# Attention and mixture of experts on one core: unit loads cut in two and tied to places of TensorE's step, two pieces of the routing moved on VectorE

## The chip, the cores and the metric

The kernel runs on one core of one Trainium2 chip. The metric is the device time of one execution in microseconds (us). Before the change three runs took 606.4, 601.0 and 603.85 us, a median of 603.85 us. The profiled execution took 600.04 us, and its span from the first to the last instruction is 598.2 us.

## The reference

The reference has two halves. The first is attention for batch 8, 8 heads, sequence 576 and head size 64, in float32. Heads 0 to 3 look at a local window (the last 32 positions), heads 4 to 7 at a strided set (earlier positions with the same remainder by 32). The second is a mixture of 8 experts over the 4608 tokens: logits from a gate matrix and a bias by modality, the expert with the largest logit, its softmax weight, and a two-layer network with ReLU.

```python
rel = pos[:, None] - pos[None, :]
mask_local = (rel >= 0) & (rel < stride)
mask_strided = (rel >= 0) & (pos[None, :] % stride == pos[:, None] % stride)
...
logits = x @ w_gate + modality_bias[modality_id]
e_idx = np.argmax(logits, axis=1)
...
h = np.maximum(x[mask] @ w1[e], 0.0)
out[mask] = gate_w[mask, None] * (h @ w2[e])
```

## The kernel before

**Attention.** The work is cut into 32 units that alternate between `Local` (one local head of two batches) and `Strided` (two strided heads of one batch). A software pipeline at L1093 to L1122 runs step n over them. In step n TensorE gets, in an order written out by hand (`tc.manual_schedule` for PE): the scores of unit n, the turn (transposes) of unit n-2, the masks of unit n+1 and the values of unit n-3. The `prep` of unit n+2 (L306, L400: copies of the queries into a padded tile on VectorE and ScalarE, pinned in program order) comes after that. After a batch pair's eight units, `finish_pair` and `route` are generators from which `pop(POPS)` takes five pieces a step; what a piece gives TensorE stands between the steps. Each pair's routing thus falls into the steps of the next pair. The last pair's falls into the expert stage.

**Loads.** All unit loads are issued from SP. A `Local` unit has one load of 592 KB for queries and keys (`qk`, L296) and one of 585 KB for values (`vv`, L301); a `Strided` unit has 576 KB (`qks`, L390) and 288 KB (`vs`, L395). Query and key tiles have two buffers for each kind of unit, so the load of unit n+3 can start when the scores of unit n-1 are done. The values of unit n-1 wait, from n = 3 on, for the last transpose of unit n-3 (`point`, L1099). The scheduler may move these loads on SP, except the first values, which are pinned.

**Routing.** `route` adds up logits on TensorE (L523, L528), turns them (L537), and then on VectorE finds the largest logit and the one-hot expert (L549 to L564). ScalarE takes the exponentials (L565), VectorE their sum and its reciprocal (L567, L568, L571) and a scan (L575). After 11 pieces TensorE computes ranks (`rk`, L579), VectorE the positions (L582 to L586), the expert counts (`new`, `fst`, `stp`, `cnt`, L588 to L594) and one-hot tables (L604). GpSimd multiplies `hv` (L613), and TensorE gathers the entry table (`en`, L619). Engines other than TensorE get their order from the scheduler's own timeline, except where instructions are pinned.

**Experts.** From step 28 on, GpSimd looks up entries (L810), gathers tokens (L793) and weights (L825) in a fixed order of transfers. The first slot's tokens are transposed after step 33 (L1121, `turn(0)`, L217). Twelve slots of 384 tokens and a half slot then run two layers on TensorE (L957, L971).

Of the kernel before, what the change touches and what calls it, by code (L numbers as in the profile page):

```python
# [38 lines left out]
FILL = {2: 4, 3: 6}  # L39
SETUP = 6  # L40
POPS, POPF = 5, 3
LT, RK = 7, 11
LAG = 2
PLANE, SEND, SPLIT, TURN = 1, 3, 6, 4
WHEN = {1: 0, 3: 1, 5: 2, 7: 3}
# [138 lines left out]
def attention_moe(ctx: ExitStack, tc: tile.TileContext, a, out):  # L184
# [72 lines left out]
    fst = cp.tile([P, NBP, E], BF16, name="fst")  # L257
    stp = cp.tile([P, NBP, E], BF16, name="stp")

    outs = _Group(tc, "outs")  # L260
    pace = [None]

# [24 lines left out]
    class Local:  # L287
# [2 lines left out]
        def __init__(self, bp, h, xt):  # L290
            self.bp, self.h, self.xt, self.n = bp, h, xt, 4 * bp + h

        def load(self):
            n = self.n
            self.qk = lp.tile([P, 37, 32], F32, tag="qk", name=f"qk{n}")
            nc.sync.dma_start(self.qk.rearrange("p i q -> p (i q)"), a["qkl"][self.bp, self.h])  # L296

        def load_values(self):
            n = self.n
            self.vv = lp.tile([P, 18, D + 1], F32, tag="vv", name=f"vv{n}")  # L300
            ins = nc.sync.dma_start(self.vv.rearrange("p i c -> p (i c)"), a["vl"][self.bp, self.h])  # L301
            if n < 2:
                pin(ins)
            return ins

        def prep(self):  # L306
            self.qd = qd = qds[self.n % 2]
# [12 lines left out]
        def scores(self):  # L320
            n, qk, qd = self.n, self.qk, self.qd
            mx = lp.tile([P, 9], F32, tag="mx", name=f"mx{n}")
            self.ex = ex = lp.tile([P, 11, 64], F32, tag="ex", name=f"ex{n}")
            for g0, gn, s in self.ss:
                for g in range(gn):
                    for jj in range(2):
                        i = _place(g0 + g, jj)
                        nc.tensor.matmul(
                            s[64 * jj:64 * jj + 64, g, :],
                            qd[:, i, :, :].rearrange("p b q -> p (b q)"),  # L330
                            qk[:, 18 + i:20 + i, :].rearrange("p b q -> p (b q)"),
                            start=False, stop=True, skip_group_check=True,
                        )
                m = mx[:, g0:g0 + gn]
                nc.vector.tensor_reduce(m, s, AX.X, ALU.max)  # L335
                nc.vector.tensor_tensor(ex[:, g0:g0 + gn, :], s, m.unsqueeze(2).to_broadcast([P, gn, 64]), ALU.subtract)
                nc.scalar.activation(ex[:, g0:g0 + 4, :], ex[:, g0:g0 + 4, :], AF.Exp, scale=0.125)
            nc.scalar.activation(ex[:, 9:11, :], ex[:, 8:9, :].to_broadcast([P, 2, 64]), AF.Exp, scale=0.125)
# [16 lines left out]
        def values(self):  # L355
            n, et, vv, xt, h = self.n, self.et, self.vv, self.xt, self.h
            for bb in range(2):
                gn = 5 - bb
                o = pa(f"o{n}{bb}")[:, :(D + 1) * gn].rearrange("p (g c) -> p g c", g=gn)
                for k in range(4):  # L360
                    for jj in range(2):
                        u = 4 * k + 2 * jj + bb
                        nc.tensor.matmul(  # L363
                            o[64 * jj:64 * jj + 64, k, :], et[:, u, :, :].rearrange("p g q -> p (g q)"), vv[:, u, :],
                            start=True, stop=True, skip_group_check=True,
                        )
                if bb == 0:
                    for b2 in range(2):
                        nc.tensor.matmul(
                            o[64 * b2:64 * b2 + 64, 4, :], et[:, 16 + b2, :, :].rearrange("p g q -> p (g q)"),  # L370
                            vv[:, 16 + b2, :], start=True, stop=True, skip_group_check=True,
                        )
                rs = lp.tile([P, 5], F32, tag="rs", name=f"rs{n}{bb}")
                nc.vector.tensor_scalar(rs[:, :gn], o[:, :, D], 1e-9, None, ALU.add)
                nc.vector.reciprocal(rs[:, :gn], rs[:, :gn])
                mark(nc.vector.tensor_tensor(
                    xt[:, 5 * bb:5 * bb + gn, D * h:D * h + D], o[:, :, 0:D],
                    rs[:, :gn].unsqueeze(2).to_broadcast([P, gn, D]), ALU.mult,
                ))

    class Strided:
# [2 lines left out]
        def __init__(self, b, pr, xc):  # L384
            self.b, self.pr, self.xc, self.n = b, pr, xc, 2 * b + pr

        def load(self):
            n = self.n
            self.qk = qk = lp.tile([P, 2, S], F32, tag="qks", name=f"qks{n}")
            nc.sync.dma_start(qk.rearrange("p s t -> p (s t)"), a["qks"][self.b, self.pr])  # L390

        def load_values(self):
            n = self.n
            self.vs = lp.tile([72, 8, 2, D], F32, tag="vs", name=f"vs{n}")
            ins = nc.sync.dma_start(self.vs.rearrange("p g h d -> p (g h d)"), a["vs"][self.b, self.pr])  # L395
            if n < 2:
                pin(ins)
            return ins

        def prep(self):  # L400
            self.qz = qz = qzs[self.n % 2]
# [9 lines left out]
        def scores(self):  # L411
            n, qz, s = self.n, self.qz, self.s
            for i in range(16):
                for j in range(2):
                    r = (i // 4) * 8 + j * 4 + i % 4
                    nc.tensor.matmul(
                        s[64 * j:64 * j + 36, 18 * i:18 * i + 18],
                        qz[:, r, :, :].rearrange("p h q -> p (h q)"),
                        self.qk[:, 1, 18 * r:18 * r + 18],
                        start=False, stop=True, skip_group_check=True,  # L420
                    )
# [12 lines left out]
            nc.vector.tensor_scalar(sm[:], sm[:], 1e-9, None, ALU.add)  # L434
            nc.vector.reciprocal(sm[:], sm[:])
            self.en = lp.tile([P, 16, 18], F32, tag="ens", name=f"ens{n}")
            nc.vector.tensor_tensor(self.en[:], ex[:], bc(sm), ALU.mult)

        def turn(self):
            n = self.n  # L440
# [12 lines left out]
        def values(self):  # L453
            n, eb, vs, b = self.n, self.eb, self.vs, self.b
            for g2 in range(2):
                ot = pa(f"ot{n}{g2}")[:, :288]
                for g in (2 * g2, 2 * g2 + 1):
                    for j in range(2):
                        c = (g % 2) * 144 + 72 * j
                        for h in range(2):  # L460
                            nc.tensor.matmul(  # L461
                                ot[64 * h:64 * h + 64, c:c + 72],
                                vs[:, 2 * g + j, h, :],
                                eb[:, 2 * g + j, :, 18 * h:18 * h + 18],
                                start=True, stop=True, skip_group_check=True,
                            )
                base = (b % 2) * S
                dst = self.xc[:, base:base + S].rearrange("p (q r) -> p r q", r=32)[:, 16 * g2:16 * g2 + 16, :]
                mark(nc.scalar.copy(dst, ot.rearrange("p (r q) -> p r q", r=16)))
# [47 lines left out]
    def route(bp, xt, xcs):  # L517
# [45 lines left out]
        ohb = ap.tile([P, E, 9], BF16, tag="ohb", name=f"ohb{bp}")  # L563
        nc.vector.tensor_copy(ohb.rearrange("p e t -> p t e"), oh[:])  # L564
        nc.scalar.activation(lo[:], lo[:], AF.Exp)  # L565
        sm = ap.tile([P, 9], F32, tag="sml", name=f"sml{bp}")
        nc.vector.tensor_reduce(sm[:], lo[:], AX.X, ALU.add)  # L567
        nc.vector.tensor_scalar(sm[:], sm[:], 1e-9, None, ALU.add)  # L568
        val = ap.tile([P, 9, 2], F32, tag="val", name=f"val{bp}")
        nc.gpsimd.tensor_copy(val[:, :, 0], tok[:, 9 * bp:9 * bp + 9])  # L570
        nc.vector.reciprocal(val[:, :, 1], sm[:])  # L571

        cum = ap.tile([P, E, 9], BF16, tag="cum", name=f"cum{bp}")
        ohf, cuf = ohb.rearrange("p e t -> p (e t)"), cum.rearrange("p e t -> p (e t)")
        nc.vector.tensor_tensor_scan(cuf, ohf, ohf, float(T2 * bp // P), ALU.add, ALU.bypass)  # L575
        for _ in range(RK):
            yield
        rk = pa(f"rk{bp}")[:, 0:72]
        nc.tensor.matmul(rk, cb[:, M_TRI:M_TRI + P], ohf, start=True, stop=False)  # L579
# [4 lines left out]
        nc.vector.tensor_reduce(pos[:], po[:], AX.X, ALU.add)  # L584
        posi = ap.tile([P, 9], I32, tag="posi", name=f"posi{bp}")
        nc.vector.tensor_copy(posi[:], pos[:])  # L586
        new = ap.tile([P, E], BF16, tag="new", name=f"new{bp}")
        nc.vector.tensor_tensor(new[:], cum[:, :, 0], ohb[:, :, 0], ALU.subtract)  # L588
        nc.vector.tensor_tensor(fst[:, bp, :], new[:], cnt[:, bp, :], ALU.subtract)
        if bp:  # L590
            nc.vector.tensor_tensor(stp[:, bp, :], fst[:, bp, :], fst[:, bp - 1, :], ALU.subtract)
        else:
            nc.vector.tensor_copy(stp[:, 0, :], new[:])
        nc.vector.tensor_tensor(cnt[:, bp + 1, :], cum[:, :, 8], fst[:, bp, :], ALU.subtract)  # L594
        pa_i = ap.tile([P, 9], I32, tag="pai", name=f"pai{bp}")
        nc.vector.tensor_single_scalar(pa_i[:], posi[:], 5, ALU.arith_shift_right)
        pa_f = ap.tile([P, 9], F32, tag="paf", name=f"paf{bp}")
# [486 lines left out]

    nu = len(units)
    for i in range(3):
        units[i].load()
        if i < 2:
            units[i].prep()
    man = tc.manual_schedule(engines={mybir.EngineType.PE})  # L1090
# [1 line left out]
    units[0].masks()  # L1092
    for n in range(nu + 3):  # L1093
        if n + 3 < nu:
            units[n + 3].load()
        if 1 <= n <= nu:
            ins = units[n - 1].load_values()
            if n >= 3:
                after_landing(ins, units[n - 3].point)  # L1099
        if n in FILL:  # L1100
            keep_busy(FILL[n], f"warm{n}")
        if n < nu:
            units[n].scores()
        if 2 <= n <= nu + 1:
            units[n - 2].turn()
        if n + 1 < nu:
            units[n + 1].masks()
        if n >= 3:
            units[n - 3].values()
            if n - 3 in ends:  # L1110
                extra.append(after(*ends[n - 3]))
        if n == SETUP:
# [82 lines left out]
```

## Time and profile before

| | |
|---|---|
| median of the three runs | 603.85 us |
| profiled execution | 600.04 us, span 598.2 us |
| TensorE busy | 575.0 us, 96% of the span |
| VectorE, ScalarE, GpSimd busy | 383.5, 329.1, 196.0 us |
| granted TensorE clock, mean | 0.977 |
| moved by DMA | 103.50 MB, 173 GB/s on average |

In the profile PE is TensorE, PEld its weight loads, DVE VectorE, ACT ScalarE, POOL GpSimd and SP the engine that issues the unit loads. A granted clock of 1.00 is 2.4 GHz and 0.50 is 1.2 GHz. "issue" is idle time in which an engine waited for nothing that the profile shows. A DMA queue of the kind "instruction" carries none of the kernel's tensors.

### The profile page before, as it was taken

The numbers are of one execution on the slowest core, as the hardware profiler recorded it, in microseconds if no ns is written. First come the engines' busy times: TensorE is split into PE (matmuls) and PEld (weight loads), VectorE is DVE, ScalarE is ACT, GpSimd is POOL, SyncE is SP. The second block draws the span as 40 slices with busy tenths as digits, with TensorE's granted clock in tenths as the row PEclk, the third lists the DMA queues.
The fourth block names the chain that finished last, engine by engine and source line by source line (L and its number), as shares of the span: only waits on it lengthen the run. The fifth ranks groups of instructions, "written<-read, shape, count | busy, mean of one in ns | idle before, by whom it ended". The sixth has DMA issues, their size and how long they took to land.

```text
span 598.2 us, 13646 instructions
## 1 busy us (share of the span) xinstructions
PE 575.0 (96%) x5461; PEld 508.9 (85%) x5461; DVE 383.5 (64%) x925; ACT 329.1 (55%) x656; POOL 196.0 (33%) x194
## 2 busy tenths in 40 slices
PE   8699899889999999999999999999999999999995
PEld 4687797767889899999899898999999898998984
DVE  6666785976886795455476766657476666655432
ACT  5668868777684353545355544536454454545442
POOL 3010210201645425532254444444434444423121
PEclk9979989999799999999999999999999999999998
DMA  8976896986779424654554155332414156422421
GB/s 307 298 237 204 292 310 230 346 261 211 238 273 349 151 79 157 231 176 176 158 195 107 53 195 157 128 72 69 91 35 107 53 194 159 156 54 106 159 89 56
DMA packets 52635, 103.50 MB, mean 173 GB/s; under 512 B 32659, under 2 KB 32915, under 8 KB 48468
## 3 DMA queue, kind: packets, MB, share of 16 engines
q0 software_dynamic: 15904, 57.47, 27.6%
q1 hardware_dynamic: 33780, 39.85, 22.6%
q10 hardware_dynamic: 2880, 5.23, 2.5%
q8 instruction: 45, 0.74, 0.5%
q14 instruction: 26, 0.21, 0.1%
HBM read 98.28 MB, written 19.18 MB: 196 GB/s over the span
## 4 chain that ended last, share of the span: by engine, by line
PE 72%; issue 1%; DVE 1%; ACTq 0%; POOL 0%; ACT 0%; POOLq 0%
PE h L957 34%; PE o L971 33%; PE xt L217 1%; PE o L363 1%; PE ot L461 0%; PE hh L880 0%; PE lg L523 0%; PE xs L217 0%; PE en L619 0%; PE xl L217 0%; ACTq L513 0%; PE ts L217 0%; PE t L217 0%; POOL out L979 0%; DVE mx L335 0%
## 5 line engine op out<-in xcount | busy, mean ns | idle before, releaser
L993 DVE TENSOR_TENSOR wl<-raw,wh 128x512 fp32r<-128x512 f32 x192 | 126.2, 695 | 86.4 <-ACT wh L992 86.2
L992 ACT CAST wh<-raw 128x512 fp32r<-128x512 f32 x192 | 109.4, 620 | 115.3 <-PE o L971 108.8
L957 PE MATMUL h<-xh,wl 128*128 128x384 f32 x384 | 129.5, 337 | 0.0
L957 PE MATMUL h<-xl,wh 128*128 128x384 f32 x384 | 129.0, 336 | 0.0
L957 PE MATMUL h<-xh,wh 128*128 128x384 f32 x384 | 128.1, 337 | 0.0
L971 PE MATMUL o<-wh,hl 128*128 128x512 f32 x288 | 113.7, 395 | 0.0
L971 PE MATMUL o<-wl,hh 128*128 128x512 f32 x288 | 113.5, 394 | 0.0
L971 PE MATMUL o<-wh,hh 128*128 128x512 f32 x288 | 112.8, 392 | 0.0
L960 ACT ACTIVATE hh<-h 128x384 fp32r<-128x384 f32 x96 | 47.2, 492 | 87.0 <-PE h L957 86.9
L962 DVE SCALAR_TENSOR_TENSOR hl<-h,hh 128x384 fp32r<-128x384 f32 x96 | 53.3, 555 | 58.2 <-ACT hh L960 57.9
L825 POOL DMA_INDIRECT raw<-in_w,wi x48 | 55.9, 1165 | 80.3 <-ACT hh L960 70.5
L957 PEld LDWEIGHTS h<-xh,wh 128*128 128x128 f32 x384 | 72.2, 188 | 3.9
L957 PEld LDWEIGHTS h<-xl,wh 128*128 128x128 f32 x384 | 72.1, 188 | 3.7 <-issue 0.4
L957 PEld LDWEIGHTS h<-xh,wl 128*128 128x128 f32 x384 | 72.0, 188 | 0.0
L793 POOL DMA_INDIRECT fx<-xd,le x36 | 37.8, 1051 | 81.7 <-DMA work<-work 21.4
L971 PEld LDWEIGHTS o<-wh,hl 128*128 128x128 f32 x288 | 54.0, 188 | 11.5
L971 PEld LDWEIGHTS o<-wl,hh 128*128 128x128 f32 x288 | 54.1, 188 | 9.3
L971 PEld LDWEIGHTS o<-wh,hh 128*128 128x128 f32 x288 | 54.1, 188 | 8.9
L810 POOL DMA_INDIRECT le<-ld,li x36 | 37.8, 1051 | 57.1 <-DVE lo L556 25.7
L979 POOL DMA_INDIRECT out<-y,le x36 | 37.5, 1041 | 44.0 <-ACT y L978 38.3
L515 POOL DMA_DIRECT2D xd<-xt x10 | 7.2, 722 | 64.8 <-ACT xt L478 40.7
L920 DVE COPY work<-fx 128x1536 uint16<-128x1536 uint16 x16 | 27.2, 1743 | 0.0
(192 smaller groups left out, 781.1 us busy)
## 6 DMA issues: line engine op xcount, KB each, us to landing
qk<-in_qkl SPq DMA_DIRECT2D x16, 592.0 KB
vv<-in_vl SPq DMA_DIRECT2D x16, 585.0 KB
qks<-in_qks SPq DMA_DIRECT2D x16, 576.0 KB
vs<-in_vs SPq DMA_DIRECT2D x16, 288.0 KB
xd<-xt POOLq DMA_DIRECT2D x8, 512.0 KB, 6.9
xd<-xt ACTq DMA_DIRECT2D x4, 1024.0 KB
raw<-in_w,wi POOLq DMA_INDIRECT x48, 4.5
le<-ld,li POOLq DMA_INDIRECT x36, 4.2
```

Source lines behind the costliest of these rows:

```text
L515: in_turn(nc.gpsimd.dma_start(dst, xt[:, k0:k0 + kn, :]))
L793: ins = in_turn(nc.gpsimd.indirect_dma_start(xt[:, h, :], None, xd[0:xrows, :], IOA(ap=le[:, h, 0:1], axis=0), **bounds))
L810: in_turn(nc.gpsimd.indirect_dma_start(le[:, h, :], None, ld[0:1 + last, :], IOA(ap=li[:, s, h:h + 1], axis=0)))
L825: ins = nc.gpsimd.indirect_dma_start(raws[j].rearrange("p f c -> p (f c)"), None, a["w"], IOA(ap=wi[:, s, j:j + 1], axis=0), bounds_check= ...
L920: pin(nc.vector.tensor_copy(rows[:, :, w, :], halves(xt)[:, :, :, w]))
L957: nc.tensor.matmul(hp, w[:, a1], x[:, c, :], start=(k == 0), stop=(k == 11))
L960: steps.append(nc.scalar.activation(hh[:], hp, AF.Relu))
L962: nc.vector.scalar_tensor_tensor(hl[:], hp, 0.0, hh.bitcast(F32), ALU.max, ALU.subtract)
L971: nc.tensor.matmul(os[h], hx[:, m], w[:, 512:1024], start=(f == 0 and i == 0), stop=(f == 7 and i == 2))
L979: outs.add(in_turn(nc.gpsimd.indirect_dma_start(out, IOA(ap=le[:, h, 0:1], axis=0), y[:], None, bounds_check=NT - 1, oob_is_err=False), True))
L992: nc.scalar.copy(wh[:, c], raw[:, c])
L993: nc.vector.tensor_tensor(wl[:, c], raw[:, c], wh[:, c].bitcast(F32), ALU.subtract)
```

## The change

Each unit load is cut in two, and both halves get a place in the step on SP, pinned in program order. The first half of unit n+3 (its queries) is issued at the top of step n, which is behind the previous step's last load. The second half (its keys) waits for the last score matmul of unit n. The first half of unit n-1's values waits for the last transpose of unit n-2. The second half waits for the last value matmul of unit n-3. A `Strided` unit's values stay in one piece, in the first of those two places.

In the routing the sum of exponentials with its reciprocal, and the four expert counts, leave their places. They stand together nine pieces behind the scan and two ahead of the ranks. `behind_units` orders the sum and the first count on VectorE behind the last strided unit's normalised exponents (`ens`, L437) recorded so far, without a semaphore.

```diff
+LT, RS, RK = 7, 9, 11
...
+    def behind_units(ins):
+        if spots:
+            tc.add_manual_dep(ins.ins, spots[-1].ins.name, behind, reason="units first")
...
-        def load(self):
-            self.qk = lp.tile([P, 37, 32], F32, tag="qk", name=f"qk{n}")
-            nc.sync.dma_start(self.qk.rearrange("p i q -> p (i q)"), a["qkl"][self.bp, self.h])
+        def load(self, part):
+            if part == 0:
+                self.qk = lp.tile([P, 37, 32], F32, tag="qk", name=f"qk{n}")
+            c = slice(0, 18 * 32) if part == 0 else slice(18 * 32, 37 * 32)
+            return pin(nc.sync.dma_start(
+                self.qk.rearrange("p i q -> p (i q)")[:, c], a["qkl"][self.bp, self.h, :, c]))
...
+            c = slice(9 * part * (D + 1), 9 * (part + 1) * (D + 1))
+            return pin(nc.sync.dma_start(
+                self.vv.rearrange("p i c -> p (i c)")[:, c], a["vl"][self.bp, self.h, :, c]))
...
+            return pin(nc.sync.dma_start(self.qk[:, part, :], a["qks"][self.b, self.pr, :, S * part:S * part + S]))
...
+            spots.append(nc.vector.tensor_tensor(self.en[:], ex[:], bc(sm), ALU.mult))
...
         nc.vector.tensor_tensor_scan(cuf, ohf, ohf, float(T2 * bp // P), ALU.add, ALU.bypass)
-        for _ in range(RK):
+        for _ in range(RS):
+            yield
+        sm = ap.tile([P, 9], F32, tag="sml", name=f"sml{bp}")
+        behind_units(nc.vector.tensor_reduce(sm[:], lo[:], AX.X, ALU.add))
+        nc.vector.tensor_scalar(sm[:], sm[:], 1e-9, None, ALU.add)
+        nc.vector.reciprocal(val[:, :, 1], sm[:])
+        new = ap.tile([P, E], BF16, tag="new", name=f"new{bp}")
+        behind_units(nc.vector.tensor_tensor(new[:], cum[:, :, 0], ohb[:, :, 0], ALU.subtract))
...
+        for _ in range(RK - RS):
             yield
...
         if n + 3 < nu:
-            units[n + 3].load()
-        if 1 <= n <= nu:
-            ins = units[n - 1].load_values()
-            if n >= 3:
-                after_landing(ins, units[n - 3].point)
+            units[n + 3].load(0)
         if n in FILL:
             keep_busy(FILL[n], f"warm{n}")
         if n < nu:
             units[n].scores()
+        if n + 3 < nu:
+            after_landing(units[n + 3].load(1), units[n].scored)
         if 2 <= n <= nu + 1:
             units[n - 2].turn()
+        if 1 <= n <= nu:
+            ins = units[n - 1].load_values(0)
+            if n >= 2:
+                after_landing(ins, units[n - 2].point)
         if n + 1 < nu:
             units[n + 1].masks()
         if n >= 3:
             units[n - 3].values()
+        if 1 <= n <= nu:
+            ins = units[n - 1].load_values(1)
+            if ins and n >= 3:
+                after_landing(ins, units[n - 3].valued)
```

## Rows read from the trace of the kernel before

**Rows 1.** Stretches: length, busy us (count) by engine, granted clock, DMA share, GB/s.
```profile
17.66:28.40 10.74, 7.09 (x203) 6.35 (x200) 8.77 (x28) 7.81 (x18) 0.00 (x0) 1.00 0.99 321
28.40:38.70 10.30, 9.47 (x149) 8.26 (x150) 3.57 (x9) 5.07 (x12) 2.64 (x6) 0.50 0.70 216
72.80:79.60 6.80, 6.09 (x81) 5.38 (x82) 6.08 (x23) 3.17 (x7) 2.06 (x3) 0.50 0.96 370
151.30:158.10 6.80, 6.36 (x100) 5.39 (x96) 6.07 (x27) 3.64 (x10) 4.31 (x5) 0.50 0.67 185
158.10:574.00 415.90, 415.90 (x2263) 376.07 (x2261) 261.78 (x491) 205.89 (x379) 167.45 (x155) 1.00 0.45 144
```

**Rows 2.** TensorE's waits, 0 to 170 us: waiter, releaser: total us, times, longest.
```profile
PE s L328 <- issue: 4.1, 3, 3.2
PE ts L217 <- DVE ens L437: 3.6, 3, 1.7
PE ts L217 <- issue: 1.5, 1, 1.5
PE ss L416 <- issue: 1.4, 2, 1.3
```

**Rows 3.** TensorE in order of time: start, us, what, matmuls, idle before it.
```profile
22.11 0.34 PE L461 MATMUL ot<-eb,vs 72*64 72x72 f32 x3 [1.33 <-issue]
...
25.39 0.69 PE L328 MATMUL s<-qk,qd 128*64 128x64 f32 x17
29.23 1.33 PE L328 MATMUL s<-qk,qd 128*64 128x64 f32 x19 [3.16 <-issue]
...
39.11 1.22 PE L328 MATMUL s<-qk,qd 128*64 128x64 f32 x36
...
43.83 0.60 PE L217 MATMUL ts<-cf_sb,ens 128*72 128x128 f32 x4 [0.43 <-DVE ens L437]
...
45.70 1.21 PE L328 MATMUL s<-qk,qd 128*64 128x64 f32 x35
...
107.49 0.27 PE L328 MATMUL s<-qk,qd 128*64 128x64 f32 x2 [0.63 <-issue]
...
114.25 0.27 PE L363 MATMUL o<-vv,et 128*64 128x65 f32 x1 [0.20 <-issue]
...
161.60 1.53 PE L217 MATMUL xt<-cf_sb,fx 128*128 128x128 f32 x12
```

**Rows 4.** DMA packets in 20.8 to 26.6 us; then, last two, 26.6 to 27.9.
```profile
DMA packets 415, 1.68 MB, mean 289 GB/s; under 512 B 49, under 2 KB 49, under 8 KB 414
...
DMA packets 146, 0.45 MB, mean 344 GB/s; under 512 B 26, under 2 KB 58, under 8 KB 145
q8 instruction: 1, 0.02, 5.1%
```

**Rows 5.** The page's DMA issues: KB each and median us to landing.
```profile
xd<-xt POOLq DMA_DIRECT2D x8, 512.0 KB, 6.9
...
fx<-xd,le POOLq DMA_INDIRECT x36, 4.4
```

**Rows 6.** VectorE in order of time, around the first and third routing.
```profile
66.62 0.23 DVE L567 TENSOR_REDUCE sml<-lo 128x9 f32<-128x72 f32 x1 [1.18 <-ACT lo L565]
...
69.25 0.16 DVE L588 TENSOR_TENSOR new<-cum,ohb 128x8 bf16<-128x8 bf16 x1
...
72.91 0.46 DVE L437 TENSOR_TENSOR ens<-exs,sms 128x288 f32<-128x288 f32 x1
...
147.52 0.23 DVE L567 TENSOR_REDUCE sml<-lo 128x9 f32<-128x72 f32 x1 [1.83 <-ACT lo L565]
```

**Rows 7.** In order of time: a load's issue, a prep, a token gather.
```profile
30.64 0.35 SPq L296 DMA_DIRECT2D qk<-in_qkl  x1
...
42.59 0.44 DVE L311 COPY qd<-qk 64x576 f32<-64x576 f32 x1
...
154.44 1.00 POOL L793 DMA_INDIRECT fx<-xd,le  x1 [0.36 <-DMA le<-ld,li]
```

More of the change, by code (lines that the diff above doesn't have):

```diff
@@ L41 @@
 POPS, POPF = 5, 3
-LT, RK = 7, 11
+LT, RS, RK = 7, 9, 11
 LAG = 2
@@ L258, in attention_moe @@
     stp = cp.tile([P, NBP, E], BF16, name="stp")
+    spots = []
+    def behind_units(ins):
+        if spots:
+            tc.add_manual_dep(ins.ins, spots[-1].ins.name, behind, reason="units first")
     outs = _Group(tc, "outs")
@@ L291, in __init__, with load_values @@
             self.bp, self.h, self.xt, self.n = bp, h, xt, 4 * bp + h
-        def load(self):
+        def load(self, part):
             n = self.n
-            self.qk = lp.tile([P, 37, 32], F32, tag="qk", name=f"qk{n}")
-            nc.sync.dma_start(self.qk.rearrange("p i q -> p (i q)"), a["qkl"][self.bp, self.h])
-        def load_values(self):
-            n = self.n
[L300 to L304, printed above, removed]
+            if part == 0:
[3 more added lines that the diff above has]
+                self.qk.rearrange("p i q -> p (i q)")[:, c], a["qkl"][self.bp, self.h, :, c]))
+        def load_values(self, part):
+            n = self.n
+            if part == 0:
+                self.vv = lp.tile([P, 18, D + 1], F32, tag="vv", name=f"vv{n}")
+            c = slice(9 * part * (D + 1), 9 * (part + 1) * (D + 1))
+            return pin(nc.sync.dma_start(
+                self.vv.rearrange("p i c -> p (i c)")[:, c], a["vl"][self.bp, self.h, :, c]))
         def prep(self):
@@ L327, in scores @@
                         i = _place(g0 + g, jj)
-                        nc.tensor.matmul(
+                        self.scored = nc.tensor.matmul(
                             s[64 * jj:64 * jj + 64, g, :],
@@ L362, in values @@
                         u = 4 * k + 2 * jj + bb
-                        nc.tensor.matmul(
+                        self.valued = nc.tensor.matmul(
                             o[64 * jj:64 * jj + 64, k, :], et[:, u, :, :].rearrange("p g q -> p (g q)"), vv[:, u, :],
@@ L385, in __init__, with load, load_values @@
             self.b, self.pr, self.xc, self.n = b, pr, xc, 2 * b + pr
-        def load(self):
+        def load(self, part):
             n = self.n
[L389 to L398, printed above, removed]
+            if part == 0:
+                self.qk = lp.tile([P, 2, S], F32, tag="qks", name=f"qks{n}")
+            return pin(nc.sync.dma_start(self.qk[:, part, :], a["qks"][self.b, self.pr, :, S * part:S * part + S]))
+        def load_values(self, part):
+            if part == 0:
+                self.vs = lp.tile([72, 8, 2, D], F32, tag="vs", name=f"vs{self.n}")
+                return pin(nc.sync.dma_start(
+                    self.vs.rearrange("p g h d -> p (g h d)"), a["vs"][self.b, self.pr]))
         def prep(self):
@@ L415, in scores @@
                     r = (i // 4) * 8 + j * 4 + i % 4
-                    nc.tensor.matmul(
+                    self.scored = nc.tensor.matmul(
                         s[64 * j:64 * j + 36, 18 * i:18 * i + 18],
@@ L436, in scores @@
             self.en = lp.tile([P, 16, 18], F32, tag="ens", name=f"ens{n}")
-            nc.vector.tensor_tensor(self.en[:], ex[:], bc(sm), ALU.mult)
+            spots.append(nc.vector.tensor_tensor(self.en[:], ex[:], bc(sm), ALU.mult))
         def turn(self):
@@ L460, in values @@
                         for h in range(2):
-                            nc.tensor.matmul(
+                            self.valued = nc.tensor.matmul(
                                 ot[64 * h:64 * h + 64, c:c + 72],
@@ L565, in route @@
         nc.scalar.activation(lo[:], lo[:], AF.Exp)
-        sm = ap.tile([P, 9], F32, tag="sml", name=f"sml{bp}")
-        nc.vector.tensor_reduce(sm[:], lo[:], AX.X, ALU.add)
-        nc.vector.tensor_scalar(sm[:], sm[:], 1e-9, None, ALU.add)
         val = ap.tile([P, 9, 2], F32, tag="val", name=f"val{bp}")
         nc.gpsimd.tensor_copy(val[:, :, 0], tok[:, 9 * bp:9 * bp + 9])
-        nc.vector.reciprocal(val[:, :, 1], sm[:])
         cum = ap.tile([P, E, 9], BF16, tag="cum", name=f"cum{bp}")
@@ L575, in route @@
         nc.vector.tensor_tensor_scan(cuf, ohf, ohf, float(T2 * bp // P), ALU.add, ALU.bypass)
-        for _ in range(RK):
+        for _ in range(RS):
[6 more added lines that the diff above has]
+        behind_units(nc.vector.tensor_tensor(new[:], cum[:, :, 0], ohb[:, :, 0], ALU.subtract))
+        nc.vector.tensor_tensor(fst[:, bp, :], new[:], cnt[:, bp, :], ALU.subtract)
+        if bp:
+            nc.vector.tensor_tensor(stp[:, bp, :], fst[:, bp, :], fst[:, bp - 1, :], ALU.subtract)
+        else:
+            nc.vector.tensor_copy(stp[:, 0, :], new[:])
+        nc.vector.tensor_tensor(cnt[:, bp + 1, :], cum[:, :, 8], fst[:, bp, :], ALU.subtract)
+        for _ in range(RK - RS):
             yield
@@ L586, in route @@
         nc.vector.tensor_copy(posi[:], pos[:])
[L587 to L594, printed above, removed]
         pa_i = ap.tile([P, 9], I32, tag="pai", name=f"pai{bp}")
@@ L1086, in attention_moe @@
     for i in range(3):
-        units[i].load()
+        for part in range(2):
+            units[i].load(part)
         if i < 2:
@@ L1109, in attention_moe @@
             units[n - 3].values()
+        if 1 <= n <= nu:
+            ins = units[n - 1].load_values(1)
+            if ins and n >= 3:
+                after_landing(ins, units[n - 3].valued)
+        if n >= 3:
             if n - 3 in ends:
```

## The prediction

> **What bounds the kernel now.** I read the stretches first. From 158.1 us to the end of the expert stage TensorE is busy 415.9 of 415.9 us at a granted clock of 1.00 [rows 1]: nothing that the change touches can shorten that stage, only let it begin earlier. All there is to win lies in the first 160 us, the attention. There the same view shows three stretches at a granted clock of 0.50, one of the two levels (1.2 instead of 2.4 GHz): 28.4 to 38.7, 72.8 to 79.6 and 151.3 to 158.1 us. Next I read TensorE's waits. Two kinds lead: "issue", 4.1 + 1.5 + 1.4 us and a single one of 1.33, 8.3 us together, and 3.6 us for `ens` on VectorE [rows 2, 3]. Then I read TensorE in order of time, to see what an "issue" wait is. The wait of 1.33 us before 22.11 and that of 3.16 us before 29.23 stand in the middle of matmuls of one kind, 17 into a group of 36 in the second case. Between the two I counted 126 matmuls in the same view; between the waits before 107.49 and 114.25, where other work runs, 126 again [rows 3]. A wait that comes back after a fixed count, whatever the work, is not a wait for data. The DMA view names it: a queue of the kind "instruction" sends one packet of 0.02 MB at 26.6 to 27.9 us, just before TensorE goes on at 29.23, and none in the 5.8 us before, when 1.68 MB of loads went by [rows 4]. I conclude that TensorE's next block of instructions stood behind the unit loads; in that stretch the DMA engines were busy 0.99 of the time [rows 1]. The clock fell at 28.4 us, while TensorE sat in this wait.
>
> **Cost of a slow stretch.** A pair of steps from 39.11 to 45.70 took 6.59 us at full clock, with a wait of 0.43 us for `ens` in it: 6.16 [rows 3]. The pair before took 13.72, and 10.56 without its wait of 3.16 [rows 3]. So the 10.3 us at 0.50 cost 4.4 us, 0.43 us for each us. By that ratio the two of 6.8 us cost 2.9 us each.
>
> **Part one: loads in halves.** It adds 40-odd issues on SP at 0.35 us each [rows 7], at most four a step of about 3.1 us (half of 6.16), so 1.4 us: SP itself hides them. Bytes stay the same. What changes is how much of them stands in line at once. Today `qk` and `vv` (592 and 585 KB) go out one right behind the other, 1177 KB; after it no place issues over about 590 KB (the second half of `vv` and the next unit's first half), and the second half of a key load goes a step later than now.
>
> - Early steps: 1.33 + 3.16 + 4.4 = 8.9 us at most. A pair of steps loads 592 + 585 + 576 + 288 = 2041 KB, and at the 321 GB/s of 17.66 to 28.40 [rows 1] that takes 6.5 us against 6.16 of matmuls. The DMA engines remain nearly full here, and some of the wait returns as a shorter one. Ends: 0 (the line stays as long as now) and 8.9. I take 6.0, two thirds, since the deep clock loss needs a long wait and the 3.16 is the only one.
> - The other "issue" waits: 8.3 - 4.5 = 3.8 us over the later steps. GpSimd's stores of 512 KB [rows 5] remain in line there. Ends 0 and 3.8; I take 2.5.
>
> The Trainium skill (Runtime: NRT & Kernel Launch, Instruction fetch mechanics) says that crossing from one block of instructions to the next costs a DMA tail bump that is mostly hidden. The trace disagrees where the loads are dense; by the page part one would be worth 0, and the sum 7.1 instead of 14.6 us.
>
> **Part two: the sum and the counts on VectorE.** In the first routing VectorE stands for 1.18 us in front of `sml`, waiting for ScalarE's exponentials, with the unit's work queued behind it; `ens` comes at 72.91 and TensorE has waited 1.7 us for it [rows 2, 6]. After the change `sml` runs when those exponentials are long done. The three operations of the sum and the four counts, 0.15 to 0.33 us each and about 0.8 us together since neighbours overlap, stand behind `ens`. So `ens` comes 1.18 + 0.8 = 2.0 us earlier, which is more than the 1.7.
>
> - First two routings: 1.7 + 1.5 of the 3.6 us go (the rest is the 0.43 at 43.83). With the first wait the slow stretch at 72.8 should go, 2.9 us. Ends 0 and 6.1. VectorE has 6.08 us busy of 6.80 in that stretch [rows 1] and is late next, now for the masks' maxima and the position arithmetic, so I take 4.6.
> - Third routing: VectorE waits 1.83 us for the same exponentials [rows 6], and 2.9 us of clock are lost behind it. But the first slot's tokens come next: the last gather is issued at 154.44 and takes 1.00 + 4.4 us [rows 5, 7], so it lands near 159.8, and its transposes run at 161.60 [rows 3]. No more than 1.8 us can be won. Ends 0 and 1.8; I take 1.5.
> - Fourth routing: it lies in the expert stage, which has no idle TensorE time: nothing, at either end.
> - What uses the moved results: `hv` needs the sum, but waits longer for the table `hb`; the counts are ready earlier than before for the slots' tables. Nothing waits anew.
>
> **What the new waits cost.** SP stands in its fixed order behind scores, transposes and values. Behind a waiting half are the next halves, on SP alone. The first half's reader is `prep`, pinned on VectorE and ScalarE. Today the load of 30.64 is read at 42.59 [rows 7], four steps later; the half will be released two steps before its `prep`, about 6.2 us at full pace. A 512 KB transfer lands in 6.9 us by the median, a gather in 4.4 [rows 5]. A half of 296 KB without stores beside it should be nearer to the second. Ends: 0 and 11 us (second rival); I take 1.0.
>
> **Sum.** 6.0 + 2.5 + 4.6 + 1.5 - 1.0 = 13.6 us. The profiled execution of 600.04 us would become 586.4. It is 3.8 us below the median of the runs, so the median goes from 603.85 to about 590.5 us.
>
> **The rivals.**
>
> 1. *The line is as long as before* (0.18). Halves change the order, not the bytes, and with the DMA engines 0.99 busy the instruction packet may stand behind as much as now; or the "issue" waits have another cause, as the page's rule would have it. Against: the packet came right before TensorE went on. Then only part two remains: 4.6 + 1.5 = 6.1 us less 1.0, about 598.7 us.
> 2. *Loads come too late: slower* (0.09). Place: `prep` at L311 and L405. It decides once a half takes over 6.2 us from release to landing. Then VectorE and ScalarE stand at each `prep` by the excess, up to 6.9 - 6.2 = 0.7 us a step, in the 16 steps where the DMA engines are full (up to 29 and around 98 to 124 us): 11 us, and the line does not shorten. With part two's 6.1 us that is +5, and with one more slow stretch +3 to +4: about 612 us. For: the lead halves. Against: the loads that were late so far stood behind 1177 KB. The Trainium skill (DMA: Bandwidth & Descriptors, Rules for kernel authors) advises at least 1 MiB per DMA for full bandwidth, which speaks for this rival; no row here times such halves.
> 3. *VectorE is the next bound* (0.13). Part one works, but in the routing steps VectorE is as full as TensorE and `ens` stays late by another way, so the clock falls at 72.8 as before. Then 6.0 + 2.5 + 1.0 - 1.0 = 8.5 us: 595 us.
>
> **How the numbers follow.** The forecast has 0.60, with its own range 582.5 to 597: all upper ends give 8.9 + 3.8 + 6.1 + 1.8 = 20.6 us, and half the sum some 7. A measurement tells about 1%, 6 us, from no change. Faster by over 1% (below 597.8) hold nearly all of the forecast, the third rival and a third of the first: 0.76. Slower by over 1% holds the second, 0.08. Within 1%: 0.16. The range is 582.5 to 600.5: it takes in the first rival's time, and leaves out the second and the tails.
>
> **What would show it.** Right: no "issue" wait over 1.5 us before 40 us, and a granted clock of 1.00 from 28 to 39 us; `sml` with no idle time ahead of it; `ts` waits for `ens` under 1 us in all; the first token transposes near 148 us instead of 161.60, the expert stage as long as before. Wrong, if "issue" waits keep their 8 us, if VectorE or ScalarE is idle behind `qk` or `qks` at `prep`, or if TensorE waits for the tokens `fx` by more than it saved before.

## The result, and the profile after

The changed kernel takes 598.66 us (median of 20 runs, 594.05 to 605.99), the kernel before 606.04 us beside it (20 runs, 601.0 to 611.3). The ratio is **0.9901 [0.9877, 0.9925]**: 1.0% faster, 6 us, where the forecast was 13.6. The time lies inside the range, and it is nearly to the digit that of the first rival (598.7). That match is luck in part: the rival took 5.1 us off a median of 603.85, and what was measured is 6 us off 606.04. The profiled execution after took 598.07 us, that of before 600.04, which is less than any of the 20 timed runs of before. So the pair of profiles shows only 2 of the 6 us, and no row of it alone can be held against the median.

**The stretches** of the changed kernel (columns as in [rows 1]):

```profile
17.00:28.00 11.00, 8.25 (x240) 7.47 (x236) 9.25 (x31) 8.29 (x18) 0.00 (x0) 1.00 0.99 306
28.00:39.00 11.00, 10.34 (x294) 9.07 (x289) 8.90 (x27) 9.80 (x23) 2.87 (x6) 1.00 0.82 248
120.00:130.00 10.00, 8.83 (x164) 7.88 (x164) 6.68 (x43) 6.79 (x16) 0.00 (x0) 0.83 0.61 192
...
150.00:160.00 10.00, 8.47 (x131) 7.15 (x125) 6.52 (x25) 4.71 (x11) 6.91 (x7) 0.83 0.82 257
170.00:575.00 405.00, 405.00 (x2088) 367.02 (x2088) 250.43 (x436) 194.48 (x353) 166.79 (x147) 1.00 0.44 138
```

From 28 to 39 us the clock is 1.00 now, where it was 0.50 for 10.3 us [rows 1]; two stretches of 3.4 us at 0.50 are left, near 123 and 154 us. The expert stage is as full as before.

**TensorE's waits**, 0 to 170 us (columns as in [rows 2]):

```profile
PE s L338 <- issue: 5.4, 5, 2.2
PE o L373 <- issue: 3.5, 2, 2.4
PE ot L470 <- DMA vs<-in_vs: 3.3, 2, 2.4
PE en L630 <- POOL hv L624: 1.2, 1, 1.2
...
PE ss L425 <- issue: 1.2, 3, 0.5
PE ot L470 <- issue: 1.1, 2, 0.8
PE ts L217 <- DVE ens L446: 0.6, 1, 0.6
PE ts L217 <- DVE sml L584: 0.5, 1, 0.5
```

The routing's wait went as forecast: 3.6 us for `ens` became 1.1 for `ens` and `sml`. The "issue" waits did not fall: 5.4 + 3.5 + 1.2 + 1.1 = 11.2 us. And there is a wait that did not exist, 3.3 us for a strided unit's values.

**TensorE in order of time** (columns as in [rows 3]) shows where they stand:

```profile
21.56 0.34 PE L470 MATMUL ot<-eb,vs 72*64 72x72 f32 x3 [0.85 <-issue]
27.39 0.80 PE L338 MATMUL s<-qk,qd 128*64 128x64 f32 x19 [1.86 <-issue]
...
73.08 1.43 PE L470 MATMUL ot<-eb,vs 72*64 72x72 f32 x31 [2.44 <-DMA vs<-in_vs]
80.14 0.46 PE L373 MATMUL o<-vv,et 128*64 128x65 f32 x9 [2.40 <-issue]
...
121.17 0.34 PE L338 MATMUL s<-qk,qd 128*64 128x64 f32 x5 [2.16 <-issue]
...
153.86 2.14 PE L630 MATMUL en<-hv,ha 128*36 128x64 f32 x18 [1.21 <-POOL hv L624]
...
158.20 1.53 PE L217 MATMUL xt<-cf_sb,fx 128*128 128x128 f32 x12
...
163.74 0.44 PE L968 MATMUL h<-xh,wh 128*128 128x384 f32 x1 [0.28 <-ACT wh L1003]
```

The early waits shrank, 1.33 and 3.16 us [rows 3] to 0.85 and 1.86, and the first token transposes start 3.4 us earlier. The wait before 27.39 is still one for instructions. The DMA view from 24.5 to 27.6 us has the instruction packet again, and the four microseconds ahead of it have none (queue: packets, MB, share of the time of the 16 DMA engines):

```profile
DMA packets 430, 0.93 MB, mean 301 GB/s; under 512 B 49, under 2 KB 49, under 8 KB 428
...
q1 hardware_dynamic: 428, 0.91, 96.4%
q8 instruction: 1, 0.02, 2.6%
```

**The new wait** in order of time, on VectorE and on SP:

```profile
66.08 0.46 DVE L446 TENSOR_TENSOR ens<-exs,sms 128x288 f32<-128x288 f32 x1
66.45 0.22 DVE L584 TENSOR_REDUCE sml<-lo 128x9 f32<-128x72 f32 x1
...
74.27 0.45 DVE L321 COPY qd<-qk 64x576 f32<-64x576 f32 x1 [1.24 <-DMA qk<-in_qkl]
```

```profile
64.25 0.37 SPq L406 DMA_DIRECT2D vs<-in_vs  x1
64.72 1.79 SPq L305 DMA_DIRECT2D qk<-in_qkl  x2
```

`sml` now stands behind `ens` with no idle time, as the change means it to. But the values issued at 64.25 are first used at 73.08, 8.8 us later and 2.4 us too late, and VectorE waits 1.24 us in a `prep` for a half, the sign of the second rival. Three other such waits, near 41, 44 and 79 us, are under 0.3 us. The DMA engines are full around it (stretches, columns as in [rows 1]):

```profile
60.00:70.00 10.00, 9.46 (x261) 8.40 (x260) 9.97 (x45) 9.11 (x22) 2.17 (x3) 1.00 0.98 317
70.00:80.00 10.00, 5.28 (x133) 4.52 (x132) 5.87 (x18) 6.55 (x16) 1.94 (x3) 1.00 0.99 338
```

### The profile page after: what moved, and what is told of

Same layout as the page of the kernel before. It is cut to its first block, busy times and chain, and to the rows that moved or that the text cites. A ratio compares the mean times of both kernels' runs of the same rounds, so it can differ in the third digit from the quotient of the medians.

```text
span 596.3 us, 13716 instructions
## 1 busy us (share of the span) xinstructions
PE 570.7 (96%) x5461; PEld 504.6 (85%) x5461; DVE 383.9 (64%) x925; ACT 328.8 (55%) x656; POOL 203.5 (34%) x194
## 3 DMA queue, kind: packets, MB, share of 16 engines
q1 hardware_dynamic: 40692, 39.85, 23.6%
## 4 chain that ended last, share of the span: by engine, by line
PE 88%; issue 4%; DMA 4%; ACT 2%; POOL 1%; DVE 1%; POOLq 0%; ACTq 0%
PE h L968 34%; PE o L982 33%; DMA vs<-in_vs 3%; PE s L338 2%; PE ot L470 2%; PE ss L425 2%; PE o L373 2%; PE xs L217 2%; PE lg L532 1%; PE warm L204 1%; PE t L217 1%; PE xl L217 1%; PE xt L217 1%; DMA le<-ld,li 1%; PE ts L217 1%
## 5 line engine op out<-in xcount | busy, mean ns | idle before, releaser
L804 POOL DMA_INDIRECT fx<-xd,le x36 | 44.3, 1231 | 82.0 <-DMA work<-work 21.4
L821 POOL DMA_INDIRECT le<-ld,li x36 | 39.0, 1082 | 58.1 <-DVE lo L565 26.0
```

What stands on the lines that cost most here:

```text
L804: ins = in_turn(nc.gpsimd.indirect_dma_start(xt[:, h, :], None, xd[0:xrows, :], IOA(ap=le[:, h, 0:1], axis=0), **bounds))
L821: in_turn(nc.gpsimd.indirect_dma_start(le[:, h, :], None, ld[0:1 + last, :], IOA(ap=li[:, s, h:h + 1], axis=0)))
```

## The experiments

**The budget of a trace.** TensorE's losses in the first 170 us can be added up for each profiled execution: the "issue" waits, the waits for the routing on VectorE (`ens`, `sml`, `pos`), the waits for unit loads, and the time at clock 0.50 times the 0.43 us per us worked out ahead. All in us:

| kernel | issue | routing | loads | at 0.50 | sum | span | span - sum |
|---|---|---|---|---|---|---|---|
| before | 8.5 | 4.0 | 0 | 23.9 | 22.8 | 598.2 | 575.4 |
| before, again | 11.2 | 4.2 | 0 | 13.7 | 21.3 | 598.5 | 577.2 |
| loads alone (second) | 9.0 | 4.3 | 1.1 | 17.1 | 21.8 | 597.7 | 575.9 |
| routing alone | 12.2 | 2.0 | 0.9 | 13.7 | 21.0 | 598.4 | 577.4 |
| routing alone (second) | 14.1 | 2.2 | 0 | 3.4 | 17.8 | 595.9 | 578.1 |
| after | 11.2 | 1.1 | 3.3 | 6.8 | 18.5 | 596.3 | 577.8 |
| after, again | 8.9 | 1.9 | 2.3 | 10.2 | 17.5 | 594.1 | 576.6 |
| after, third | 10.0 | 1.8 | 1.0 | 20.5 | 21.6 | 596.3 | 574.7 |
| late stores | 8.5 | 2.6 | 0.6 | 13.7 | 17.6 | 595.8 | 578.2 |
| whole loads, two places | 12.8 | 1.9 | 0 | 20.5 | 23.5 | 600.4 | 576.9 |
| strided values early | 12.1 | 2.4 | 1.6 | 13.7 | 22.0 | 599.0 | 577.0 |
| no values | 0.2 | 3.1 | 0 | 0 | 3.3 | 581.7 | 578.4 |
| no values, again | 2.6 | 2.0 | 1.5 | 3.4 | 7.6 | 583.7 | 576.1 |
| no values, old routing | 5.6 | 4.1 | 0.8 | 17.1 | 17.9 | 593.7 | 575.8 |

The last column stays between 574.7 and 578.4 while the span moves by 18.7 us. So these four losses are the story to within 2 us, the ratio of 0.43 included. (The kernel of the seventh experiment, with 580.2, also waits 3.9 us for ScalarE. The first profile of the loads alone, of the longest of its executions, is left out.) Two profiles of one kernel differ by up to 4.3 us in their sum, so the table shows which kind of loss a change moves, and the timed ratios show how much.

**1. Which part does it.** The two theories were that the halves shorten the line in which instruction blocks stand, and that only bytes count in that line. The kernel before was profiled again, each part ran alone, and the values were left out.

> The kernel before, profiled a second time. Its profile on record took 600.04 us, under every one of the 20 timed runs (601.0 to 611.3, median 606.04). If that profile was a good draw, this one shows more than 8.3 us of issue waits on TensorE before 170 us, or more than 24 us at a granted clock of 0.50. If it was typical, both repeat within 1 us.

The second profile has four stretches of 3.4 us at 0.50 in place of 10.3, 6.8 and 6.8, and "issue" waits of 11.2 us in place of 8.5; its time is 600.39 us. The wait of 3.16 us near 29 us is 1.25 us here. What I had read as the kernel's own 10.3 us was one draw.

> The halves and their places alone; the routing as before. Theory (both parts work, each smaller than forecast): about half of the 6 to 7 us, a ratio of 0.993 to 0.997 to the kernel before, with ens waits of 3 us as before. Rival (the line on the DMA engines is not shortened, all the gain is part two's): 0.999 to 1.004.

```diff
-    sum and counts behind the strided exponents
+    sum and counts at their places before (loads in halves kept)
```

1.0002 [0.9978, 1.0026]: nothing. The rival's range holds it, the theory's does not.

> The routing's sum and counts behind the unit's exponents alone; loads whole as before. Theory: the other half, 0.993 to 0.997, ens waits under 1 us, issue waits as before. Rival (part two is all): 0.988 to 0.991.

```diff
-    units[n + 3].load(0) ... units[n + 3].load(1)
+    units[n + 3].load()      # whole loads of before; routing of after kept
```

1.0039 [1.0009, 1.0069]: no gain either, so that both the theory and the rival missed. The routing's waits are halved (2.0 us), but "issue" is 12.2 us.

> The changed kernel without its value loads from the third unit on: every unit reads the first values of its kind again, so 42% of the unit loads' bytes go and the output is another. Theory (TensorE's instruction blocks stand in line behind the loads): issue waits before 150 us fall from 11 us to under 3 us, no wait for vs, no slow stretch before 120 us, and 8 to 14 us less time than the changed kernel. Rival (issue waits have another cause): issue waits stay at 8 us or more, and only the 3.3 us of vs waits go.

```diff
+            if "vv" in kept and kept["vv"][1] is not self:
+                self.vv = kept["vv"][0]
+                return None
...
+            if "vs" in kept:
+                self.vs = kept["vs"]
+                return None
```

0.9739 [0.9686, 0.9791], 583.21 us. A pair of steps now loads 592 + 576 = 1168 KB instead of 2041. Its stretches, and its waits, 0 to 170 us:

```profile
17.00:28.00 11.00, 10.17 (x278) 9.10 (x275) 9.94 (x34) 9.27 (x20) 0.00 (x0) 1.00 0.78 225
28.00:39.00 11.00, 9.83 (x304) 8.74 (x302) 9.85 (x28) 10.18 (x25) 2.64 (x6) 1.00 0.68 219
```

```profile
PE ts L217 <- DVE sml L593: 2.1, 3, 1.0
...
PE ot L479 <- issue: 0.2, 1, 0.2
```

With the DMA engines at 0.78 instead of 0.99 the "issue" waits are gone, and the clock is 1.00 to the end of the attention. All that is left is 0.23 us in front of the same three matmuls where 1.33 us stood [rows 3]. That those waits are blocks of instructions that stand behind loads, as the prediction had it, fits this run; what cures them is fewer bytes. The packet records bear it out. In the 13 profiles with all loads there are 88 "issue" waits of 0.3 us or more before 140 us, and each of them ends 1.2 to 1.6 us after a 16 KB packet of the queue q8 of the kind "instruction" has ended. Some 25 such packets come by 160 us, so most of them have no wait behind them.

**2. Can the new wait be taken away?** On another chip, beside the whole change:

> The changed kernel once more, beside the kernel before on the chip of this call. In the call before, the kernel before took 597.83 us (median of 23) where the result on record has 606.04, and each part alone was worth nothing. Theory (the gain on record hangs on the draw of how the instruction blocks meet the line, so on the chip too): ratio 0.995 to 1.003 here if the kernel before is again near 598. Rival (the two parts need each other): 0.988 to 0.993 whatever the chip.

0.9959 [0.9927, 0.9992]: the gain here is 0.4%, not 1.0%. It lies in the theory's range.

> The changed kernel with the strided values released a step earlier (top of the step, behind the last transpose of unit n-3, as before the change). Theory (the value loads' later place made the new waits of 3.3 us for vs): no wait for vs over 0.5 us, 2 to 4 us less than the changed kernel. Rival (the DMA engines are full, so another load or an instruction block comes later by as much): within 1 us of the changed kernel.

```diff
+        early = 1 <= n <= nu and isinstance(units[n - 1], Strided)
+        if early:
+            ins = units[n - 1].load_values(0)
+            if n >= 3:
+                after_landing(ins, units[n - 3].point)
```

0.9987 [0.9951, 1.0022]. The wait for `vs` is gone, and the next block of instructions takes its place. TensorE in order of time:

```profile
73.88 1.22 PE L470 MATMUL ot<-eb,vs 72*64 72x72 f32 x31 [0.84 <-issue]
83.31 0.70 PE L373 MATMUL o<-vv,et 128*64 128x65 f32 x9 [4.73 <-issue]
```

2.44 + 2.40 us after; 0.84 + 4.73 here. That is the rival's mechanism: the order of the line chooses which reader waits. Its price of within 1 us isn't settled, since the two ratios on this chip, 0.9987 and 0.9959, lie 1.7 us apart with intervals of 2 us to each side.

> The changed kernel with whole loads again, pinned at the two first places (queries and keys at the top of the step, values behind the transposes of unit n-2). Theory (the size of the pieces matters little, the backlog counts): within 2 us of the changed kernel, issue waits 9 to 13 us. Rival (halves shorten the line, as forecast): 3 to 6 us slower than the changed kernel, issue waits longer by as much.

```diff
-            c = slice(0, 18 * 32) if part == 0 else slice(18 * 32, 37 * 32)
+            if part:
+                return None
+            c = slice(0, 37 * 32)
```

0.9959 [0.9925, 0.9992], the same ratio as the whole change on that chip. The theory held: whole loads at the two first places do as well as halves at four. What the pinned places are worth without the halves was not run beside the routing alone on one chip.

> The changed kernel with GpSimd's chain of look-ups, gathers and weights begun at step 27 instead of 28. Theory (at the end of the attention TensorE waits for this chain: hv 1.2 us, first weights): 1 to 3 us less than the changed kernel. Rival (the chain is not the last): within 1 us, or slower since its transfers join the line.

```diff
-EARLY, BEGIN = 2, 28
+EARLY, BEGIN = 2, 27
```

1.0058 [1.0027, 1.0089]: slower than before. With GpSimd's lookups and gathers a step earlier the DMA engines are busy 0.97 of the time from 140 to 150 us, where the changed kernel has 0.82, so that they seem to join the line. TensorE's waits from 100 to 170 us begin with

```profile
PE o L373 <- DMA vv<-in_vl: 4.0, 2, 3.8
```

**3. What the routing is worth where the line is short.**

> The changed kernel without its value loads from the third unit on (the output is another), as a base for the next run on the same chip: issue waits under 1 us before 150 us, ratio to the kernel before 0.972 to 0.980.

0.9664 [0.9618, 0.9709], 585.97 us on this chip. Both numbers missed: the gain is larger than expected, and the "issue" waits are 2.6 us in all.

> The same without value loads, and with the routing of the kernel before (sum and counts in their old places). Theory (part two's gain is refunded as longer issue and load waits only where the DMA engines are full): with light loads part two's worth shows whole, so this one is 2.5 to 6 us slower than the run before it, with 3 us or more of ens waits. Rival (part two is worth nothing by itself): within 1 us of it.

```diff
-        for _ in range(RS):
-            yield
-        sm = ...; behind_units(...); new = ...; behind_units(...)
+        for _ in range(RK):      # sum and counts at their places before
```

0.9836 [0.9789, 0.9883], 596.61 us. TensorE's order shows the old wait, unchanged, in both routings (1.7 us was the longest in [rows 2]):

```profile
64.98 1.04 PE L217 MATMUL ts<-cf_sb,ens 128*72 128x128 f32 x4 [1.69 <-DVE ens L455]
...
104.03 0.60 PE L217 MATMUL ts<-cf_sb,ens 128*72 128x128 f32 x4 [1.69 <-DVE ens L455]
```

So with light loads part two is worth 596.61 - 585.97 = 10.6 us, 1.8%: by the table 2.1 us of routing waits, 3.0 of "issue" waits and 13.7 us less at 0.50 (5.9 us), less 0.7 for loads: 10.3 of the 10.0 us between the spans. That is more than the 2.5 to 6 us expected, and not all of it can be laid to the routing's waits. The "issue" waits of these two runs are not those of the runs with all loads: nearly all of them stand behind 130 us, and all but one end at other distances from an instruction packet than 1.2 to 1.6 us. With the old routing they come as

```profile
142.20 0.19 PE L434 MATMUL ss<-qks,qz 128*36 128x18 f32 x1 [0.50 <-issue]
142.91 0.33 PE L434 MATMUL ss<-qks,qz 128*36 128x18 f32 x3 [0.51 <-issue]
143.66 0.38 PE L434 MATMUL ss<-qks,qz 128*36 128x18 f32 x6 [0.43 <-issue]
```

and the DMA engines were only 0.08 busy from 141 to 142 us. What they wait for isn't shown. (The first profile of the changed kernel has four such waits behind 142 us, 1.6 us of its 11.2.) These waits and the time at 0.50 behind them make 4.5 of the 10.3 us; the other 5.8 us go with the routing's own waits. With all loads the same edit was worth nothing beside whole loads, and 0.9936 / 0.9992, 0.6%, beside loads in halves (part 4).

> The changed kernel with GpSimd's stores of the first two batch pairs held back to steps 17, 18, 25 and 26, three pieces a step, out of the full stretches at 60 to 80 and 100 to 120 us. Theory (the line is the backlog, and the stores are a large part of it there): issue and vs waits between 60 and 120 us fall from some 10 us to under 5 us, 2 to 5 us less time than the changed kernel. Rival (the unit loads alone fill the line): the same waits, and the stores add new ones at steps 17 to 19 and 25 to 27: 0 to 4 us slower.

```diff
+LATE = (17, 18, 25, 26)
...
-        if stores:
-            stores.pop(0)()
+        if n in LATE or n > 26:
+            for _ in range(3):
+                if stores:
+                    stores.pop(0)()
```

0.9915 [0.988, 0.995] on that chip, against 0.9901 [0.9877, 0.9925] of the change itself on record: no better. The changed kernel was not run beside it on this chip. Between 60 and 120 us the "issue" and `vs` waits fell to 4.3 us, as the theory had it, where the changed kernel has 6.8; the wait for `vs` is gone, and the longest is one of 2.6 us for instructions. The time did not follow.

**4. The parts and the whole on one chip.** Still open was whether the parts add up.

> The loads alone again, now beside the whole change and the routing alone on one chip. Theory (where the DMA engines are full a wait that goes comes back under another name, so the parts don't add): ratio 0.994 to 1.002, 10 to 12 us of issue waits.

0.9992 [0.9959, 1.0024], with 9.0 us of "issue" waits. TensorE's order shows the wait that the halves were to shorten, to the digit as before [rows 3], and the stretch behind it at the lower clock again:

```profile
28.11 0.95 PE L338 MATMUL s<-qk,qd 128*64 128x64 f32 x19 [3.16 <-issue]
...
73.18 1.04 PE L217 MATMUL ts<-cf_sb,ens 128*72 128x128 f32 x4 [1.69 <-DVE ens L446]
```

```profile
28.00:40.00 12.00, 11.89 (x203) 10.62 (x203) 5.65 (x17) 6.26 (x14) 2.64 (x6) 0.57 0.60 160
```

> The routing alone again. Theory: ratio 0.994 to 1.004, with the ens waits down by 2 us and the issue and load waits up by as much. Rival (the parts add, and the chips differ): here as much gain as the whole change less that of the loads alone.

0.9985 [0.9939, 1.0032]. TensorE's order, and the stretches:

```profile
29.91 0.80 PE L335 MATMUL s<-qk,qd 128*64 128x64 f32 x19 [3.16 <-issue]
...
69.79 0.60 PE L217 MATMUL ts<-cf_sb,ens 128*72 128x128 f32 x4 [0.54 <-DVE sml L582]
...
82.77 0.71 PE L370 MATMUL o<-vv,et 128*64 128x65 f32 x9 [4.15 <-issue]
```

```profile
28.00:40.00 12.00, 10.02 (x299) 9.02 (x300) 8.50 (x27) 8.29 (x20) 2.64 (x6) 1.00 0.86 264
80.00:90.00 10.00, 7.23 (x126) 6.69 (x127) 4.85 (x16) 3.70 (x10) 0.00 (x0) 0.83 0.77 265
```

The wait of 1.69 us at 73 us is 0.54 us, and thirteen microseconds on TensorE waits 4.15 us for instructions instead. The first profile of the routing alone has 6.8 us at 0.50 behind a wait of 2.64 us near 29 us.

> The whole change on the same chip. Theory: 0.988 to 0.997, more than the product of the two parts' ratios. Rival (the parts add): the product, within 0.002.

0.9936 [0.9909, 0.9963]. In its order of time the early wait is

```profile
27.64 0.80 PE L338 MATMUL s<-qk,qd 128*64 128x64 f32 x19 [3.00 <-issue]
```

and 6.8 us at 0.50 follow: of three profiles of the changed kernel, one has the early loss after all. The parts multiply to 0.9992 x 0.9985 = 0.9977, the whole is 0.9936. Whether it is more than its parts stays open: the two parts' intervals, some 0.003 and 0.005 wide to each side, cover the difference of 0.004. So does the size: 6.0 us on record, 2.5 and 3.8 us on two other chips.

No version tried that keeps the output beats the changed kernel.

## Why the prediction was right in direction and wrong in size

**Part one, early steps (6.0 us) and other "issue" waits (2.5 us): the step that failed.** Its cause was right and its cure was not. The waits are instruction blocks behind loads (no values: 0.2 us left). But "how much of them stands in line at once" does not set them. Loads alone gave 1.0002 and 0.9992, the second with the 3.16 us in place; whole loads at two places gave as much as halves. I had the number that points to it: 2041 KB take 6.5 us against 6.16 of matmuls. A queue that is filled faster than it is emptied keeps its line whatever the size of its pieces; "two thirds" had no row under it. In place of 8.5 us the term is about 0: the means of the profiles have "issue" waits of 9.9 us before and 10.0 after. (One reading was loose: the 5.8 us ahead of the packet do hold a packet of 0.01 MB of another instruction queue, q14, at 26.49; q8, whose packet ends ahead of TensorE's start, has none there.)

By its rule that a block's crossing is mostly hidden, the Trainium skill (Runtime: NRT & Kernel Launch, Instruction fetch mechanics) gave part one 0, which is what it was worth. The trace of the kernel before agrees by count, since 24 packets of q8 by 160 us leave 8 waits, and not by size: with all loads the "issue" waits are 5.4 to 14.1 us of a run. The sum by the page was added up wrongly: 14.6 less 8.5 is 6.1 us, not 7.1.

**Part two, first two routings (4.6 us).** The mechanism was right: the two waits for `ens`, 1.7 and 1.5 us, are 0.54 us and nothing in all three profiles of the changed kernel. Its size was near in its place (the routing's waits fell by 2.5 us by the means of the profiles, of 3.2 forecast) and wrong in what follows. A step that starts earlier also asks for its loads and its next block earlier, and these stand in the same full line. The waits fit that, 4.15 us at 82.77 with the routing alone and 2.44 + 2.40 us with both, but no run follows it load by load. So I failed to say what is late next on the DMA side; I named VectorE. With light loads the edit gave 10.6 us, of which 5.8 us can be laid to the routing's waits; its two terms had 6.1.

**Third routing (1.5 us), the cap.** Its size came out, its reason did not. The cap of 1.8 us took the last gather to stay at 154.44. It is issued at 151.16 now, and the token transposes start 3.4 us earlier (158.20 instead of 161.60). The first expert matmul starts only 1.9 us earlier, 163.74 instead of this line of before:

```profile
165.61 0.43 PE L957 MATMUL h<-xh,wh 128*128 128x384 f32 x1
```

Of the 1.5 us between, 0.28 us is a wait for the weights `wh`; the rest isn't explained. GpSimd keeps its chain of lookups and gathers, and `hv` stands behind it:

```profile
148.74 1.00 POOL L804 DMA_INDIRECT fx<-xd,le  x1 [1.58 <-ACT ex L347]
151.16 1.45 POOL L804 DMA_INDIRECT fx<-xd,le  x1 [1.42 <-DMA le<-ld,li]
152.64 1.17 POOL L624 TENSOR_TENSOR hv<-hb,val 128x576 f32<-128x576 bf16 x1
```

"Waits longer for the table `hb`" missed that: TensorE waits 1.21 us for `hv` at 153.86. (The second profile of the kernel before has 1.4 us of that wait too.) Starting the chain a step earlier does not help: 1.0058, where the change alone has 0.9959 on the same chip.

**Fourth routing (0) and the expert stage.** Right: 405.00 of 405.00 us busy at clock 1.00.

**New waits (1.0 us).** Too small. They are 3.3 us on TensorE in one profile, 2.3 and 1.0 in the others, 2.2 as a mean. I took a landing near 4.4 us for a half; the strided values, which kept their 288 KB and got a later release, took up to 8.8 us while the DMA engines were 0.98 to 0.99 busy. The second rival had loads that come too late, but in another place, `prep`, and at 11 us too high a price. The Trainium skill's rule of at least 1 MiB per DMA (DMA: Bandwidth & Descriptors, Rules for kernel authors) is not put to the test here, since no run has unit loads of that size. Below it the size did not matter: halves alone changed the time by 0.0% and -0.1%, though the loads' packets rose from 33,780 to 40,692 for the same 39.85 MB.

**The sum, as measured by the means of the profiles** (two before, three after): "issue" -0.2, routing +2.5, loads -2.2, clock 0.43 x (18.8 - 12.5) = +2.7, together 2.8 us of 13.6. On the chip of the record it was 6 us. The clock's part is an average over draws that run from 13.7 to 23.9 us at 0.50 before and from 6.8 to 20.5 after, so where the 6 us came from stays open.

**The signs named.** Held: clock 1.00 from 28 to 39 us (two profiles of three), `sml` without idle, the expert stage. Held nearly: waits for `ens` 0.6 us, under 1. Failed: no "issue" wait over 1.5 us before 40 us (1.86, 1.62 and 3.00 in the three profiles), first transposes near 148 us (158.20). The sign for wrong, "issue" waits that keep their 8 us, is what came.

## What to carry to other kernels

When loads need more time than the work they feed (6.5 us against 6.16), cutting or moving them only chose who waited here; take bytes out of that stretch, or leave it. Where several waits stand in one full line, test a fix once with the line lightened: the same routing edit gave 0 to 0.6% with all loads and 1.8% with fewer. And take a second profile of the unchanged kernel before a clock loss goes into a sum: one draw gave 23.9 us at 0.50, the next 13.7.

## What the runs showed of the hardware

- A wait's length does not fix the clock behind it. After 3.16 us of waiting near 28 us the clock was 0.50 for 10.2 us in the kernel before and with the loads alone, and 1.00 to 40 us in the second profile of the routing alone.
- The kernel before has medians of 606.04 and 606.62 us in two sets of runs and of 597.83, 598.55 and 599.5 us in three sets on other chips. The whole change gave 0.9901 beside 606.04, and 0.9959 and 0.9936 beside 598.55 and 599.5: a ratio of this size is not the same in every set. That the chip is what makes the difference is not shown, since each set was taken at one time only.
- A wait for a block of instructions can be told in a profile: it has no releaser, it comes back after a multiple of some 126 matmuls (126 between 22.11 and 29.23 before, 126 between 21.56 and 27.39 after), and it ends 1.2 to 1.6 us after a 16 KB packet in a queue of the kind "instruction".
